# Chunk 0's decays loaded by themselves, an explicit early order, and 96-column last chunks in a chunked scan with two feed-forward layers

## The chip, the cores and the metric

The kernel runs on one core of one Trainium2 chip. The metric is device time of one execution in microseconds (us). The kernel before takes 632.46 us, the median of 3 runs (632.3 to 632.98).

## The reference, cut to what matters

Three layers follow each other; each reads the whole output of the one before.

```python
# 1. scan: 4 batches, 8 heads, 768 steps, head size 32, state size 16
la  = log(clip(a, 1e-6, 1)) ; cum = cumsum(la)           # within a chunk
M   = (C @ B.T) * exp(cum_i - cum_j) * causal
y   = M @ x + (C @ state) * exp(cum)
state = exp(sum(la)) * state + sum_j B_j x_j exp(cum_last - cum_j)
# 2. 3072 tokens of 256:  g = x @ w_gate ; v = x @ w_val ; y = (silu(g) * v) @ w_out      (1536 wide)
# 3. h = x @ w_in ; y = relu(h)**2 @ w_out                                               (2048 wide)
```

## The kernel before, in words

The 768 steps of a batch are cut into 7 chunks: six of 112 steps and a last one of 96 (Q = 112; 28 chunks in all). For each chunk the kernel makes a matrix of decay products, L (a scan on VectorE over decays that TensorE has spread over the partitions, `spread` and `scan`), the scores (`scores`, tile cb), their product mt (`times`), and the chunk's output and new state in one group of 8 matmuls (`outputs`, tile ys). Ahead of the scores the inputs B and C (tile eb) are loaded, transposed by TensorE (`transpose`, tile trb) and copied out of PSUM by ScalarE in five pieces (`copy_b`, `copy_c`, tile bct). The state goes to the next chunk by a copy, a transpose (tile turn) and another copy. The chunks of one batch hang on each other by that state.

The decays `a` lie in one tile, dv: heads on partitions, chunks and steps along the row, with a zero ahead of each chunk. Two copies of it are loaded, one at partition 0 by SyncE (SP) and one at partition 64 by ScalarE's queue (`load_a`, L254 and L258), zeroed around the edges by VectorE (`zeros`, L245 to L248) and clamped in two instructions (`clip`, L264). All chunks' decays go by one load and one clamp, and the first `spread` (tile ab, L593) waits for it.

The second layer's weights are split into a high and a low part by ScalarE, VectorE and GpSimd (tile raw to v, hi, lo); its matmuls (tiles g, v, acc) run with three products each, from L764 and L878. The third layer's are h and acc (L764, L950 and L959).

The order of all work is made on the host before the program is built. The kernel adds operations with costs, dependences and priorities to a `Graph`; `order()` plays them through an event queue, at each free engine starting the available operation of the lowest priority number, and the program is issued in that order. `PLAN["turns"]` overwrites the priorities of about 510 early operations by a table of numbers. Each engine then takes its instructions strictly in this order and waits on semaphores.

Where TensorE's next operation starts more than 150 ns after the last one in that plan, the kernel puts matmuls on a tile of zeros ahead of it (tile idle, written into the next operation's own PSUM buffer, L233: "fills"). Their number is the planned gap over 105 ns, plus 2; for the first gap of the program it is another formula with the constant COLD.

Of the kernel before, what the change touches and what calls it, by code (L numbers as in the profile page):

```python
# [16 lines left out]
ALU = mybir.AluOpType  # L17
# [10 lines left out]
class Op:  # L28
    def __init__(self, eng, cost, fn, deps, prio, bufs, lat):
        self.port, self.pieces = False, 0  # L30
        self.eng, self.cost, self.fn, self.prio, self.bufs, self.lat = eng, cost, fn, prio, bufs, lat
        self.deps = [d for d in deps if d is not None]
        self.next, self.wait, self.keep = [], 0, None


class Graph:
# [14 lines left out]
    def order(self):  # L51
# [5 lines left out]
        avail, out, events, now = {}, [], [], 850.0  # L57
        busy = {}
        for op in self.ops:
            if not op.wait:  # L60
                avail.setdefault(op.eng, []).append(op)
        left = len(self.ops)
        seq = queued = 0
        while left:
            started = True
            while started:
                started = False
                for eng, ops in avail.items():
# [4 lines left out]
                    for op in ops:  # L73
                        if best is not None and (eng == "DMA" or op.prio > best.prio):
                            continue
# [6 lines left out]
                        if op.keep and "ps" in need:  # L82
                            more, own, accs = op.keep
                            need["ps"] += more + sum(len(accs[u]) for u in own if not accs[u][0].taken)
# [4 lines left out]
                    ops.remove(best)  # L89
# [20 lines left out]
            while events and events[0][0] <= now:  # L110
# [13 lines left out]
                for o in op.next:  # L124
                    if (o.eng == op.eng) == near:
                        o.wait -= 1
                        if not o.wait:
                            avail.setdefault(o.eng, []).append(o)
# [5 lines left out]
def kernel(  # L134
# [13 lines left out]
    nc = tc.nc  # L148
# [93 lines left out]
    def zeros():  # L242
        for u in range(HG):
            w = dv_all[64 * u : 64 * u + R]
            nc.vector.memset(w[:, :, 0:1], 0.0)  # L245
            if full < NCB:
                nc.vector.memset(w[:, full, 1 + S - full * Q :], 0.0)
        nc.vector.memset(dv_all[R:64], 0.0)  # L248

    def load_a(u):  # L250
# [4 lines left out]
            out=w[:, :full, 1:], in_=v[:, : full * Q].rearrange("p (c q) -> p c q", c=full)  # L255
# [3 lines left out]

    def clip():  # L260

        w = dv_all[0 : 64 + R]
        for v in (w[:, :full, 1:], w[:, full:, 1 : 1 + S - full * Q]):
            nc.vector.tensor_scalar(v, v, 1e-6, 1.0, op0=ALU.max, op1=ALU.min)  # L264
# [67 lines left out]
    op_tab = g.add("ACT", 600, act_table, prio=-940)  # L332
# [9 lines left out]
    op_zero = g.add("DVE", 1000, zeros, prio=-960)  # L342
    ld_a = [dma(q, 2, 450, 350, lambda u=u: load_a(u), [], -950) for u, q in enumerate(["SP", "ACT"])]
    op_clip = g.add("DVE", 900, clip, [*ld_a, op_zero], -950)

    def keep_decays(b):
# [5 lines left out]
        b: dma("SP", 1, 450, 200, lambda b=b: keep_decays(b), [op_clip], 300 + b if b else 100 * PLAN["kept_at"], pieces=56)  # L352
# [109 lines left out]
    def chunk_ops(k, prio, after=(), load_after=()):  # L462
# [120 lines left out]
        if early and k < C0:  # L583
# [23 lines left out]
            o = g.add("PE", 1080, spread, [op_clip, op_pick, before.scans[-1] if before else None], prio, [*pab, c.L], lat=250)  # L607
# [87 lines left out]
        def outputs():  # L695
            ps = new(psy, [P, 512], F32, "ys")
            y = ps[:, 0:256].rearrange("p (g q) -> p g q", g=HG)
            for h in range(H):
                i, j = divmod(h, G)
                nc.tensor.matmul(  # L700
                    y[j * D : (j + 1) * D, i, :], xa[k % NX][0:K, h, :], mt[0:K, h, :],
# [393 lines left out]
    for i, at in PLAN["turns"].items():  # L1095
        g.ops[i].prio = (at, i)
# [3 lines left out]
    with tc.manual_schedule():  # L1100
        for op in order:
            fills.clear()
            if op.eng == "PE":
                if op.start < PLAN["warm"]:
# [3 lines left out]
                    if gap > 150:  # L1108
                        fills.append(int(n) + PLAN["more"])
# [40 lines left out]
    turns={  # L1150
# [97 lines left out]
```

## Time and profile before

| what | value |
|---|---|
| median of 3 runs | 632.46 us |
| the profiled execution, its own time | 635.0 us |
| its span | 633.3 us |
| TensorE (PE) busy | 628.8 us, 99% |
| VectorE (DVE) busy | 430.0 us, 68% |
| ScalarE (ACT) busy | 337.6 us, 53% |
| GpSimd (POOL) busy | 103.6 us, 16% |

The profiled execution took 1.7 us more than its span, and 2.54 us more than the median of the runs. Busy time is the share in which an engine has an instruction; a fill counts as busy TensorE like any other matmul, so 99% does not mean 99% of useful work. PEld is TensorE's weight load, which runs beside its matmuls. One matmul in full 32-bit floats stands as two matmuls in the rows (8 of them are x16). Times in the rows are counted from the start of the span.

### The profile page before, as it was taken

Reading aid. Unit: us, or ns where it says so; the run is one execution under the profiler, and the core shown is the slowest. Engines: PE = TensorE matmul, PEld = TensorE weight load, DVE = VectorE, ACT = ScalarE, POOL = GpSimd, SP = SyncE. Lnnn points to the kernel's source line nnn. Section 1 sums busy time; section 2 is a strip of 40 time slices with the busy share of each in tenths; the row PEclk is TensorE's granted clock in tenths of the full one; section 3 lists DMA queues with packets and bytes.
Section 4 is the critical chain, followed back from the end, with each engine's and each line's share of the span. In section 5 each row is a group of like instructions: output and inputs, shape, how many; then the busy total and the mean of one; then the engine's idle time right before and its main releaser. Section 6 shows DMA issues by size and latency. Waiting matters only on the chain.

```text
span 633.3 us, 9819 instructions
## 1 busy us (share of the span) xinstructions
PE 628.8 (99%) x3755; PEld 532.3 (84%) x3755; DVE 430.0 (68%) x666; ACT 337.6 (53%) x615; POOL 103.6 (16%) x130
## 2 busy tenths in 40 slices
PE   9999999999999999999999999999999999999997
PEld 7889999999787878787888888888888888888897
DVE  5888889887877768794588985455555554554543
ACT  4888896454534444553467564444444444444443
POOL 4046523231312122211033310000000000000000
PEclk9999999999999999999999999999999999999999
DMA  8879764776565646533043100020010100100201
GB/s 188 204 167 221 196 158 67 137 122 140 94 138 92 133 84 113 148 77 124 1 132 134 67 1 1 0 35 0 1 33 1 26 10 1 33 1 0 35 1 34
DMA packets 153823, 49.85 MB, mean 79 GB/s; under 512 B 141616, under 2 KB 142128, under 8 KB 153776
## 3 DMA queue, kind: packets, MB, share of 16 engines
q1 hardware_dynamic: 153232, 48.87, 35.3%
q8 instruction: 29, 0.48, 0.3%
q10 hardware_dynamic: 544, 0.36, 0.2%
q14 instruction: 18, 0.15, 0.1%
HBM read 34.96 MB, written 3.25 MB: 60 GB/s over the span
## 4 chain that ended last, share of the span: by engine, by line
PE 99%; DVE 0%; issue 0%
PE h L764 21%; PE g L764 18%; PE acc L950 17%; PE acc L878 16%; PE v L764 14%; PE acc L959 4%; PE ys L700 3%; PE cb L662 2%; PE trb L233 1%; PE cb L653 1%; PE ab L593 1%; PE ab L233 1%; PE cb L233 0%; PE g L233 0%; PE trb L506 0%; PE turn L739 0%
## 5 line engine op out<-in xcount | busy, mean ns | idle before, releaser
L940 DVE TENSOR_TENSOR p<-t,p 128x512 fp32r<-128x512 f32 x96 | 67.9, 707 | 65.7 <-ACT p L936 65.7
L933 DVE TENSOR_TENSOR t<-t 128x512 f32<-128x512 f32 x96 | 66.4, 692 | 52.1 <-ACT t L930 52.0
L936 ACT ACTIVATE p<-t 128x512 fp32r<-128x512 f32 x96 | 60.7, 632 | 75.1 <-PE acc L950 53.2
L950 PE MATMUL acc<-p,hi 128*128 128x512 f32 x320 | 98.6, 389 | 0.0
L930 ACT ACTIVATE t<-h 128x512 f32<-128x512 f32 x96 | 57.4, 598 | 67.5 <-PE h L764 64.6
L878 PE MATMUL acc<-p,hi 128*128 128x512 f32 (+3 forms) x320 | 89.9, 365 | 0.0
L828 ACT ACTIVATE t<-g 128x512 f32<-128x512 f32 (+5 forms) x88 | 45.2, 519 | 73.9 <-PE g L764 66.3
L764 PE MATMUL h<-xh_all,hi 128*128 128x512 f32 x192 | 74.8, 390 | 0.0
L764 PE MATMUL h<-xl_all,hi 128*128 128x512 f32 x192 | 74.8, 390 | 0.0
L764 PE MATMUL h<-xh_all,lo 128*128 128x512 f32 x192 | 74.7, 389 | 0.0
L851 DVE TENSOR_TENSOR p<-t,p 128x512 fp32r<-128x512 f32 (+3 forms) x80 | 57.6, 731 | 21.9 <-ACT p L846 21.3
L950 PEld LDWEIGHTS acc<-p,hi 128*128 128x128 f32 x320 | 60.1, 188 | 12.5
L846 ACT ACTIVATE p<-t 128x512 fp32r<-128x512 f32 (+3 forms) x80 | 45.5, 573 | 46.9 <-DVE t L831 37.8
L764 PE MATMUL g<-xh_all,hi 128*128 128x512 f32 (+3 forms) x184 | 65.6, 356 | 0.0
L831 DVE TENSOR_TENSOR t<-t,v 128x512 f32<-128x512 f32 (+2 forms) x68 | 43.7, 646 | 31.1 <-PE v L764 23.6
L764 PE MATMUL g<-xl_all,hi 128*128 128x512 f32 (+3 forms) x184 | 64.6, 351 | 0.0
L764 PE MATMUL g<-xh_all,lo 128*128 128x512 f32 (+3 forms) x184 | 64.6, 351 | 0.0
L878 PEld LDWEIGHTS acc<-p,hi 128*128 128x128 f32 x320 | 57.2, 189 | 7.3
L950 PE MATMUL acc<-p,lo 128*128 128x512 f32 x160 | 62.2, 389 | 0.0
L878 PE MATMUL acc<-p,lo 128*128 128x512 f32 (+3 forms) x160 | 57.9, 362 | 0.0
L764 PE MATMUL v<-xh_all,hi 128*128 128x512 f32 (+2 forms) x136 | 51.1, 376 | 0.0
L764 PE MATMUL v<-xl_all,hi 128*128 128x512 f32 (+2 forms) x136 | 51.0, 375 | 0.0
(103 smaller groups left out, 1097.3 us busy)
## 6 DMA issues: line engine op xcount, KB each, us to landing
ab<-decay SPq DMA_DIRECT2D x23, 452.0 KB, 4.2
raw<-in_moe_w_out_dram SPq DMA_DIRECT2D x14, 512.0 KB, 4.6
raw<-in_moe_w_in_dram SPq DMA_DIRECT2D x8, 512.0 KB, 4.2
raw<-in_moe_w_val_dram SPq DMA_DIRECT2D x6, 512.0 KB, 5.9
raw<-in_moe_w_gate_dram SPq DMA_DIRECT2D x6, 512.0 KB, 5.4
xa<-in_x_dram SPq DMA_DIRECT2D x24, 112.0 KB, 3.0
out_dram<-o SPq DMA_DIRECT2D x40, 64.0 KB, 1.9
bc<-in_B_dram SPq DMA_DIRECT2D x18, 56.0 KB, 2.2
```

Source lines behind the costliest of these rows:

```text
L764: nc.tensor.matmul(ps, l, r, start=(i == 0), stop=(i == len(terms) - 1))
L828: nc.scalar.activation(t[:, :n], gg(), AF.Silu)
L831: nc.vector.tensor_tensor(tb.t[:, :n], tb.t[:, :n], vv(), op=ALU.mult)
L846: nc.scalar.activation(p[:, 0, :n], tb.t[:, :n], AF.Copy)
L851: e.tensor_tensor(p[:, 1, :n], tb.t[:, :n], p[:, 0, :n].bitcast(F32), op=ALU.subtract)
L878: nc.tensor.matmul(ps, l, r, start=bank not in done_f, stop=f == NF - 1, skip_group_check=True,)
L930: nc.scalar.activation(new(tb, [P, TN], F32, "t"), ph.t, AF.Relu)
L933: nc.vector.tensor_tensor(tb.t, tb.t, tb.t, op=ALU.mult)
L936: nc.scalar.activation(new(pb, [P, 2, TN], F32R, "p")[:, 0, :], tb.t, AF.Copy)
L940: e.tensor_tensor(pb.t[:, 1, :], tb.t, pb.t[:, 0, :].bitcast(F32), op=ALU.subtract)
L950: nc.tensor.matmul(acc[-1 - i][m], l.t[:, w], pb.t[:, r, :], start=(f == 0 and s == 0), stop=(f == NF2 - 1 and s == 2),)
L959: nc.tensor.matmul(acc[-1 - i][q][:, :256], pb.t[:, l, tk], r, start=(f == 0 and s == 0), stop=(f == NF2 - 1 and s == 2),)
```

## The change: what it does

Four edits.

1. Chunk 0's decays are loaded and clamped by themselves (`load_first`, `clip_first`), zeroed by a short `zeros`; the other chunks' (`load_a`, `clip`, `zeros_rest`) follow as operations of their own. Chunk 0's `spread` waits for the first alone, all other ones for the second.
2. The table of priorities goes. In its place `PLAN["seq"]` lists the early operations of each engine in order (some 400 for VectorE, 90 for GpSimd, 320 for TensorE, 360 for ScalarE, 150 for SyncE); `order()` gives an engine the next one of its list as soon as that one can run, and the rest by priority as before. The lists also rearrange the work.
3. Where a planned gap of TensorE ends at or before 12 us of the plan, the fills are now the gap over 216 ns, plus 1. Elsewhere the formulas stay. In the built program there are 64 fills where there were 137.
4. The last chunk of each batch multiplies 96 columns in `outputs` in place of 128.

```diff
-        for u in range(HG):
-            w = dv_all[64 * u : 64 * u + R]
-            nc.vector.memset(w[:, :, 0:1], 0.0)
-            if full < NCB:
-                nc.vector.memset(w[:, full, 1 + S - full * Q :], 0.0)
-        nc.vector.memset(dv_all[R:64], 0.0)
+        nc.vector.memset(dv_all[0 : 64 + R, 0, 0:1], 0.0)
+        nc.vector.memset(dv_all[R:64, 0, 1:], 0.0)
+
+    def zeros_rest():
+        w = dv_all[0 : 64 + R]
+        nc.vector.memset(w[:, 1:, 0:1], 0.0)
...
+    def load_first(u):
+        q = nc.scalar if u else nc.sync
+        q.dma_start(out=dv_all[64 * u : 64 * u + R, 0, 1:], in_=a.rearrange("b h s -> (b h) s")[:, :Q])
...
+    def clip_first():
+        v = dv_all[0 : 64 + R, 0, 1:]
+        nc.vector.tensor_scalar(v, v, 1e-6, 1.0, op0=ALU.max, op1=ALU.min)
...
-            o = g.add("PE", 1080, spread, [op_clip, op_pick, before.scans[-1] if before else None], prio, [*pab, c.L], lat=250)
+            o = g.add(
+                "PE", 1080 if k else 2000, spread, [op_clip if k else op_clip0, op_pick, before.scans[-1] if before else None],
+                prio, [*pab, c.L], lat=250,
+            )
...
+            m = n if last else P
...
-                    y[j * D : (j + 1) * D, i, :], xa[k % NX][0:K, h, :], mt[0:K, h, :],
+                    y[j * D : (j + 1) * D, i, :m], xa[k % NX][0:K, h, :], mt[0:K, h, :m],
...
-    for i, at in PLAN["turns"].items():
-        g.ops[i].prio = (at, i)
...
-                        fills.append(int(n) + PLAN["more"])
+                        fills.append(int(n) + PLAN["more"] if free < 1200 or op.start > 12000 else int(gap / 216) + 1)
...
-    turns={
-        0: 7236.6543, 1: -999.5758, 2: -999.5961, 3: -999.6149, 4: -999.5938, 5: -999.6135, 6: -999.4071, 7: -999.5258,
...
+    seq=dict(
+        DVE=[
+            10, 0, 9, 15, 40, 41, 36, 151, 35, 37, 152, 20, 155, 156, 101, 42, 174, 175, 102, 178,
...
```

SyncE's queue at the start of the program, before (dv are the decays, xa the x of a chunk, raw a pair of weight blocks of 512 KB, eb the B and C of a chunk):

```order
L254 DMA dv<-in_a_dram 32x6x112
L258 DMA dv<-in_a_dram 32x96
L484 DMA xa_92<-in_x_dram 112x8x32
L405 DMA raw<-in_moe_w_val_dram 128x2x512
L405 DMA raw<-in_moe_w_gate_dram 128x2x512
L495 DMA eb_101<-in_C_dram 112x8x16
L495 DMA eb_101<-in_B_dram 112x8x16
L405 DMA raw<-in_moe_w_val_dram 128x2x512
```

The same queue with the change, from its first load to the first chunk's x:

```order
L428 DMA raw<-in_moe_w_val_dram 128x2x512
L265 DMA dv<-in_a_dram 32x112
L428 DMA raw<-in_moe_w_gate_dram 128x2x512
L518 DMA eb_101<-in_C_dram 112x8x16
L518 DMA eb_101<-in_B_dram 112x8x16
L428 DMA raw<-in_moe_w_gate_dram 128x2x512
L271 DMA dv<-in_a_dram 32x5x112
L275 DMA dv<-in_a_dram 32x96
L518 DMA eb_102<-in_B_dram 112x8x16
L518 DMA eb_102<-in_C_dram 112x8x16
L428 DMA raw<-in_moe_w_val_dram 128x2x512
L507 DMA xa_92<-in_x_dram 112x8x32
```

One weight block moved ahead of the decays, of which only chunk 0's stand there; B and C of chunk 0 stand at places 4 and 5 in place of 6 and 7, and the x of chunk 0 went from place 3 to place 12.

VectorE around its first scan, before (the scan, of chunk 0, writes L and is named SCALAR_TENSOR_TENSOR here; v and raw are a weight block):

```order
L245 MEMSET dv 32x7
L247 MEMSET dv 32x16
L248 MEMSET dv 32x791
L264 TENSOR_SCALAR dv<-dv 96x6x112
L264 TENSOR_SCALAR dv<-dv 96x96
L602 SCALAR_TENSOR_TENSOR L<-ab,delta 128x452
L439 TENSOR_SCALAR v<-v 128x512
L433 SCALAR_TENSOR_TENSOR raw<-raw 128x512
```

And with the change:

```order
L251 MEMSET dv 96x1
L252 MEMSET dv 32x112
L279 TENSOR_SCALAR dv<-dv 96x112
L456 SCALAR_TENSOR_TENSOR raw<-raw 128x512
L462 TENSOR_SCALAR v<-v 128x512 x2
L625 SCALAR_TENSOR_TENSOR L<-ab,delta 128x452
L456 SCALAR_TENSOR_TENSOR raw<-raw 128x512
L466 SCALAR_TENSOR_TENSOR v<-v,raw 128x512
L625 SCALAR_TENSOR_TENSOR L<-ab,delta 128x452
L284 TENSOR_SCALAR dv<-dv 96x5x112
```

The clamp of chunk 0 is one instruction of 112 columns; that of the other chunks moved behind both scans of chunk 0.

## Rows read from the trace of the kernel before

**Rows 1.** The page: busy time by engine, and the chain's shares.

```profile
PE 628.8 (99%) x3755; PEld 532.3 (84%) x3755; DVE 430.0 (68%) x666; ACT 337.6 (53%) x615; POOL 103.6 (16%) x130
...
PE 99%; DVE 0%; issue 0%
```

**Rows 2.** Waits of PE from 0 to 50 us: total, times, longest (us).

```profile
PE ab L233 <- DVE idle L215: 1.1, 1, 1.1
```

**Rows 3.** Chain that ended last, 0 to 60 us: start, duration (us), engine, tile, line.

```profile
1.14 4.02 PE ab L233 x18
5.16 1.98 PE ab L593 x16
7.14 5.09 PE trb L233 x31
12.23 0.22 PE trb L506 x2
12.44 0.33 PE ab L233 x3
12.77 1.08 PE ab L593 x16
13.85 0.76 PE cb L233 x6
14.61 1.08 PE cb L653 x16
15.69 1.96 PE trb L233 x17
...
18.95 0.57 PE ys L700 x16
...
20.61 1.42 PE trb L233 x13
...
42.89 0.54 PE cb L233 x4
```

**Rows 4.** The same chain's shares of its 60 us by line.

```profile
by line: PE g L764 20.9%; PE trb L233 14.1%; PE cb L653 12.6%; PE ab L593 10.5%; PE ab L233 7.2%; PE acc L878 6.8%; PE ys L700 6.7%; PE cb L233 4.9%; PE g L233 4.7%; PE trb L506 3.3%; PE turn L739 2.3%; PE v L764 2.0%; PE turn L233 1.5%; PE
```

**Rows 5.** Issues of 3.2 to 4.6 us: KB each, us to landing.

```profile
eb<-in_C_dram SPq DMA_DIRECT2D x1, 56.0 KB, 5.5
```

**Rows 6.** The same of 0 to 1.5 us.

```profile
dv<-in_a_dram SPq DMA_DIRECT2D x1, 84.0 KB, 2.4
```

**Rows 7.** Timeline of SP: start, duration (us), queue, line.

```profile
0.82 0.40 SPq L254 DMA_DIRECT2D dv<-in_a_dram  x1
...
3.32 0.47 SPq L495 DMA_DIRECT2D eb<-in_C_dram  x1
```

**Rows 8.** Timeline of DVE, the clamp of the decays.

```profile
3.55 0.79 DVE L264 TENSOR_SCALAR dv<-dv 96x672 f32<-96x672 f32 x2
```

**Rows 9.** Timeline of ACT, chunk 0's copies out of PSUM.

```profile
12.48 0.28 ACT L510 ACTIVATE bct<-trb 128x128 f32<-128x128 f32 x1 [2.55 <-PE trb L506]
12.65 1.08 ACT L515 ACTIVATE bct<-trb,mask 128x112 f32<-128x112 f32 x4
```

**Rows 10.** Windows: PE, PEld, DVE, ACT, POOL busy, PEclk, DMA share, GB/s.

```profile
20.00:30.00 10.00, 10.00 (x120) 8.32 (x119) 8.87 (x15) 8.98 (x26) 0.83 (x2) 1.00 0.99 272
...
0.00:50.00 50.00, 48.87 (x525) 39.40 (x526) 38.70 (x65) 35.88 (x91) 17.40 (x39) 1.00 0.81 188
```

**Rows 11.** DMA of 0 to 14 us.

```profile
DMA packets 6665, 2.76 MB, mean 197 GB/s; under 512 B 5641, under 2 KB 5641, under 8 KB 6665
```

More of the change, by code (lines that the diff above doesn't have):

```diff
@@ L29, in __init__ @@
     def __init__(self, eng, cost, fn, deps, prio, bufs, lat):
-        self.port, self.pieces = False, 0
+        self.port, self.pieces, self.listed = False, 0, False
         self.eng, self.cost, self.fn, self.prio, self.bufs, self.lat = eng, cost, fn, prio, bufs, lat
@@ L56, in order @@
         free = {p: [None] * n for p, n in self.pools.items()}
-        avail, out, events, now = {}, [], [], 850.0
+        out, events, now = [], [], 850.0
         busy = {}
+        avail = {eng: [] for eng in ("DVE", "POOL", "PE", "ACT", "SP", "DMA")}
+        lists = {eng: [self.ops[i] for i in reversed(PLAN["seq"].get(eng, []))] for eng in avail}
+        for ops in lists.values():
+            for op in ops:
+                op.listed = True
         for op in self.ops:
-            if not op.wait:
-                avail.setdefault(op.eng, []).append(op)
+            if not op.wait and not op.listed:
+                avail[op.eng].append(op)
         left = len(self.ops)
@@ L72, in order @@
                     need = {}
-                    for op in ops:
-                        if best is not None and (eng == "DMA" or op.prio > best.prio):
+                    first = lists[eng][-1:]
+                    for op in first + ops:
+                        if op.listed and op.wait:
+                            continue
+                        if best is not None and (best.listed or eng == "DMA" or op.prio > best.prio):
                             continue
@@ L81, in order @@
                                 need[b.pool] = need.get(b.pool, 0) + 1
-                        if op.keep and "ps" in need:
+                        if op.keep and "ps" in need and not op.listed:
                             more, own, accs = op.keep
@@ L88, in order @@
                         continue
-                    ops.remove(best)
+                    (lists[eng] if best.listed else ops).remove(best)
                     best.after = []
@@ L126, in order @@
                         o.wait -= 1
-                        if not o.wait:
-                            avail.setdefault(o.eng, []).append(o)
+                        if not o.wait and not o.listed:
+                            avail[o.eng].append(o)
         self.span = now
@@ L242, in zeros @@
     def zeros():
-        for u in range(HG):
-            w = dv_all[64 * u : 64 * u + R]
-            nc.vector.memset(w[:, :, 0:1], 0.0)
-            if full < NCB:
-                nc.vector.memset(w[:, full, 1 + S - full * Q :], 0.0)
-        nc.vector.memset(dv_all[R:64], 0.0)
+        nc.vector.memset(dv_all[0 : 64 + R, 0, 0:1], 0.0)
[3 more added lines that the diff above has]
+        nc.vector.memset(w[:, 1:, 0:1], 0.0)
+        if full < NCB:
+            nc.vector.memset(w[:, full, 1 + S - full * Q :], 0.0)
+        nc.vector.memset(dv_all[R:64, 1:full, 1:], 0.0)
+        if full < NCB:
+            nc.vector.memset(dv_all[R:64, full, 1 : 1 + S - full * Q], 0.0)
+    def load_first(u):
+        q = nc.scalar if u else nc.sync
+        q.dma_start(out=dv_all[64 * u : 64 * u + R, 0, 1:], in_=a.rearrange("b h s -> (b h) s")[:, :Q])
     def load_a(u):
@@ L254, in load_a @@
         q.dma_start(
-            out=w[:, :full, 1:], in_=v[:, : full * Q].rearrange("p (c q) -> p c q", c=full)
+            out=w[:, 1:full, 1:], in_=v[:, Q : full * Q].rearrange("p (c q) -> p c q", c=full - 1)
         )
@@ L258, in load_a @@
             q.dma_start(out=w[:, full, 1 : 1 + S - full * Q], in_=v[:, full * Q :])
+    def clip_first():
+        v = dv_all[0 : 64 + R, 0, 1:]
+        nc.vector.tensor_scalar(v, v, 1e-6, 1.0, op0=ALU.max, op1=ALU.min)
     def clip():
         w = dv_all[0 : 64 + R]
-        for v in (w[:, :full, 1:], w[:, full:, 1 : 1 + S - full * Q]):
+        for v in (w[:, 1:full, 1:], w[:, full:, 1 : 1 + S - full * Q]):
             nc.vector.tensor_scalar(v, v, 1e-6, 1.0, op0=ALU.max, op1=ALU.min)
@@ L331 @@
     op_bc = g.add("POOL", 2200, setup_bc, prio=-900)
-    op_tab = g.add("ACT", 600, act_table, prio=-940)
+    op_tab = g.add("ACT", 1500, act_table, prio=-940)
     def dma(eng, n, cost, move, fn, deps=(), prio=0.0, bufs=(), pieces=256):
@@ L340, in dma @@
         return o
-    op_zero = g.add("DVE", 1000, zeros, prio=-960)
-    ld_a = [dma(q, 2, 450, 350, lambda u=u: load_a(u), [], -950) for u, q in enumerate(["SP", "ACT"])]
-    op_clip = g.add("DVE", 900, clip, [*ld_a, op_zero], -950)
+    op_zero = g.add("DVE", 230, zeros, prio=-999)
+    op_zrest = g.add("DVE", 980, zeros_rest, prio=-960)
+    ld_0 = [dma(q, 1, 450, 100, lambda u=u: load_first(u), [], -955, pieces=32) for u, q in enumerate(["SP", "ACT"])]
+    op_clip0 = g.add("DVE", 190, clip_first, [*ld_0, op_zero], -955)
+    ld_a = [dma(q, 2, 450, 350, lambda u=u: load_a(u), [], -950, pieces=200) for u, q in enumerate(["SP", "ACT"])]
+    op_clip = g.add("DVE", 800, clip, [*ld_a, op_zrest], -950, port=True)
     def keep_decays(b):
@@ L351 @@
     kept = {
-        b: dma("SP", 1, 450, 200, lambda b=b: keep_decays(b), [op_clip], 300 + b if b else 100 * PLAN["kept_at"], pieces=56)
+        b: dma("SP", 1, 450, 200, lambda b=b: keep_decays(b), [op_clip, op_clip0], 300 + b if b else 100 * PLAN["kept_at"], pieces=56)
         for b in range(NB)
@@ L1149 @@
     warm=70000,
-    turns={
[65 rows of a table removed]
-    },
+    seq=dict(
+        DVE=[
[21 rows of a table added]
+        ],
+        POOL=[
[5 rows of a table added]
+        ],
+        PE=[
[16 rows of a table added]
+        ],
+        ACT=[
[18 rows of a table added]
+        ],
+        SP=[
[8 rows of a table added]
+        ],
+    ),
 )
```

131 rows, old and new, of tables (ACT, DVE, PE, POOL) are left out of this document.

## The prediction, made before the changed kernel ran

> **What bounds the kernel now.** I read the page's busy times and its chain first: TensorE is busy 99% of the span and holds 99% of the chain [rows 1]. That share includes the fills, so next come TensorE's waits in the first 50 us, where all fills stand. There is one, of 1.1 us, for the tile of zeros itself [rows 2]: whatever TensorE needs has arrived before its fills are through. The others wait for it: ScalarE stood 2.55 us for chunk 0's transposes [rows 9]. So in the early stage the fills themselves set the pace. How much time they hold is read from the chain of the first 60 us: the L233 shares are 14.1 + 7.2 + 4.9 + 4.7 + 1.5 = 32.4%, or 19.4 us [rows 4]. The largest lump is 31 fills in 5.09 us ahead of chunk 0's transposes [rows 3]; the last load these wait for was issued right behind one that went out at 3.32 us and landed 5.5 us later, at 8.8 us [rows 5, 7], while the transposes began at 12.23 us. From 43.43 us on there are no fills, and the rest is matmul behind matmul; what the early stage gives up, the end gets whole.
>
> **The clock.** A fill takes 4.02 / 18 = 223 ns at the start and 1.42 / 13 = 109 ns later [rows 3]: its 256 columns at TensorE's lower level (1.2 GHz) and at the upper one (2.4 GHz). The window rows print the granted clock as 1.00 for both [rows 10], so the fills are the better witness. With 223 and 109 ns, 31 fills in 5.09 us are about 15 of the slow and 16 of the fast kind: the rise came near 10.5 us, after TensorE had run nothing but fills since 7.14 us.
>
> **The change part by part**, against the profiled execution (635.0 us, 2.54 us over the median of the runs).
>
> *To the first outputs (ys, 18.95 us).* Step by step, with the durations of before:
> - 15 fills in place of 18: 1.14 + 15 x 0.223 = 4.5 us.
> - Chunk 0's decays. Before, the SP copy went out at 0.82 us and landed 2.4 us later, at 3.2 us [rows 6, 7]. Now a 512 KB weight block stands ahead of it: at 272 GB/s with the DMA engines 99% busy [rows 10] that is 1.9 us, so 4.3 us at the least (were the block quicker) and 5.1 us at the most; I take 4.6. Clamping took 0.79 us for two instructions of 672 and 96 columns [rows 8]; one of 112 is put at 0.3 us (0.1 to 0.5). `spread` starts at 4.9 us against 5.16: 0.3 us won, or nothing. In the page DMA: Bandwidth & Descriptors, section Queues, rings and completion order, the Trainium skill says that each DMA engine consumes a queue's descriptors in ring order; by that rule the small copy can't pass the block. The sum has it so.
> - `spread` 1.98 us at the lower clock, then 3 fills of 0.22: 7.5 us, where 31 fills took the time to 12.23.
> - B and C of chunk 0: in SP's list they stand two places earlier, without the 96 KB of all decays and the 112 KB of x ahead of them. Two issues of 0.47 us are 0.9 us, and 112 KB more at 272 GB/s 0.4 us: 8.8 - 1.3 = 7.5 us (8.8 if nothing comes of it). The transposes start at 7.5 us: 4.7 us earlier, 3.4 at the least.
> - ScalarE's copies end 1.50 us after the transposes begin (12.23 to 13.73) [rows 9]; 8 fills of 0.22 us end at 9.8. Scores at 9.9 us against 14.61 [rows 3].
> - Scores 1.08 us, then 2 fills where 17 took 1.96 us, chunk 1's transposes, 3 fills, one `spread`, 7 fills: with 1.2 us for a load that is not early enough, 9.9 + 1.1 + 1.2 + 0.2 + 0.3 + 1.1 + 0.8 = 14.6 to 14.8 us against 18.95. That is **-4.2 us** (-3.0 to -5.0).
>
> *Behind the first outputs.* Of the 19.4 us, 4.02 + 5.09 + 0.33 + 0.76 + 1.96 = 12.2 us stand ahead of ys [rows 3], so 7.3 us behind it, in 62 fills. The built program has 26 there: 2.8 us at 109 ns, 3.0 with their entries. 4.3 us of fills go. What takes their place is not shown, since TensorE never waited here; the bounds are nothing (all 4.3 won) and all of it in waits (0). The cover is thin: in 20 to 30 us VectorE is busy 8.87 and ScalarE 8.98 of 10 us, and the DMA share is 0.99 [rows 10], so other engines are near their own pace as soon as TensorE stops holding them. I take half: **-2.1 us**.
>
> *96 columns.* One `outputs` is 0.57 us [rows 3]; a quarter less over four of them is at most 0.57 us, nothing at the least; the part that streams is about three quarters: **-0.4 us**.
>
> *The clock.* Fills go from the stretch in which it rose. If it rises where the second `spread` begins instead of near 10.5 us, one group of scores (1.08 us) and some transposes and fills take twice as long. I take **+1.0 us** (0 to 3.4, the latter if it stays low to about 17 us).
>
> *Rearranging behind 50 us* is taken at nothing: TensorE has its input there before it asks, and VectorE is busy 68% of the span [rows 1]. The second clamp now stands behind both scans of chunk 0 and before the scores' products, 0.8 us; chunk 1's `spread` waits for it, behind 3 fills, and that lies inside the 1.2 us above.
>
> Sum: -4.2 - 2.1 - 0.4 + 1.0 = -5.7; 635.0 - 5.7 = 629.3, less 2.54 is 626.8 us. All ends on one side give -9.9 and +0.4, or 622.6 and 632.9.
>
> **The rivals.**
> - *The loads decide* (20%). The DMA share over the first 50 us is 0.81 [rows 10]: 40 us of transfers, which can't be squeezed much. Chunk 0's x goes out behind four weight blocks and four B and C copies, about 2.5 MB; before, 2.76 MB took 14 us [rows 11]. So x lands at 13 to 14 us, hardly before ys wants it. If x comes 1 us late and all removed fills behind ys turn into waits: -3.2 - 0.4 + 1.0 = -2.6, 629.9 us. Against: nothing waits for a load before, and landings there lie 3 us ahead of use.
> - *Nothing comes back* (13%): no waits behind ys and the clock as before, -4.2 - 4.3 - 0.4 = -8.9, 623.6 us.
> - *Slower: the lower clock* (7%). TensorE stops and starts between few fills, and the rise doesn't come. From 12.23 to 43.43 us its chain holds 31.2 us, of which 19.4 - 9.1 = 10.3 us are fills; the other 20.9 us are work that takes twice as long at the lower level. Without the clock's term the sum is -6.7; the 2.1 us of waits that it holds behind ys would be filled by the longer work. So it decides from 8.8 us of such work at the lower level on. With half of the 20.9 us: 10.4 - 2.1 - 6.7 = +1.6, or 634.1 us. For it: ahead of the rise TensorE ran nothing but fills, and most of those go. Against: at the lower level the same work leaves fewer gaps between its instructions. In TensorE: Matmul & The Clock Gate, section What's actually happening, the Trainium skill says that "the default state is throttled, and activity releases the throttle". The trace agrees as far as it goes, with 223 ns a fill at first and 109 later; by that rule it speaks against the change that it takes activity away, and this rival is its price.
> - *Waits for fills, one for one* (8%): chunk 0's decays and copies come as late as before, and the time is 632 us.
>
> **How the numbers follow.** The forecast, 626.8 us with its own range of 625 to 628.5, has 52%. Faster by over 0.2% (below 631.2 us; 0.2% is about what a measurement of this kernel can tell from no change) are the forecast, the first two rivals and a little of the rest: 0.86. Within 0.2%: 0.07. Slower: 0.07. For 8 in 10 the range runs from 624.6 to 631.0.
>
> **What would show it.** L233 rows in the chain of the first 60 us at about 10 us in place of 19.4; chunk 0's transposes near 7.5 us and the first ys near 14.7; in place of the fills, waits of TensorE for ScalarE, VectorE or a DMA, about 2 us in all behind ys. Fills of over 200 ns beyond 17 us, or score groups of 2 us, would say that the clock ate the gain; a TensorE wait for xa or eb of over 1 us that the loads did. I am wrong if the transposes of chunk 0 stay later than 9 us, or if the matmuls from 50 us on start less than 3 us earlier than before.

## The result, and the profile after

The changed kernel takes 627.54 us (median of four, 627.31 to 627.66) against 632.61 us before (632.3 to 632.98): ratio 0.9913, 95% interval 0.9894 to 0.9931. Measured once more, six times against 22, it was 627.92 against 632.94, ratio 0.9916 (0.9894 to 0.9937). The prediction said 626.8 us, within 624.6 to 631.0. The time is right; several of its terms are not, and their errors nearly cancel.

The page's busy times and its chain by engine, after; they answer to [rows 1]:

```profile
PE 619.8 (99%) x3682; PEld 525.1 (84%) x3682; DVE 424.6 (68%) x668; ACT 335.2 (54%) x615; POOL 99.4 (16%) x130
PE 98%; DMA 1%; DVE 0%; SPq 0%; issue 0%; DVEq 0%
```

TensorE is still the bound; the 73 matmuls that are gone are fills (64 in place of 137). New in the chain is 1% of DMA. The chain of the first 60 us of the kernel after (start, duration, what; L241 are the fills) answers to [rows 3]:

```profile
1.32 4.41 DMA dv<-in_a_dram
...
6.19 2.05 PE ab L616 x16
8.25 0.75 PE trb L241 x3
9.00 0.43 PE trb L529 x2
9.42 1.49 PE cb L241 x8
10.91 1.08 PE cb L679 x16
...
12.86 1.08 PE ab L616 x16
13.94 0.87 PE ys L241 x7
14.81 0.57 PE ys L727 x16
...
16.46 0.76 PE turn L241 x6
...
17.66 1.08 PE ab L616 x16
18.74 1.52 PE g L241 x13
...
22.80 1.08 PE ab L616 x16
...
25.86 0.87 PE ab L241 x7
26.73 1.08 PE ab L616 x16
...
45.46 0.47 PE ys L727 x16
```

The first ys is at 14.81 us against 18.95, and the fills in the chain add up to 6.9 us (0.75 + 1.49 + 0.33 + 0.33 + 0.87 + 0.76 + 1.52 + 0.87), where there were 19.4 [rows 4]; 15 more fills lie beside the wait for chunk 0's decays. From the first ys to the end it is 625.9 - 14.81 = 611.1 us against 633.3 - 18.95 = 614.4. TensorE's waits in the first 50 us, after:

```profile
PE ab L616 <- DVE dv L279: 1.7, 1, 1.7
PE ab L241 <- DVE idle L223: 1.1, 1, 1.1
```

Against [rows 2] one wait is new, ahead of chunk 0's `spread`; behind ys there is none.

One thing can't be read from this pair alone: the two profiled executions differ by 7.4 us (635.0 and 627.6), the medians by 5.07. The first experiment shows why.

### The profile page after: what moved, and what is told of

Its sections match the earlier page's. It is cut to its first block, busy times and chain, and to the rows that moved or that the text cites. A ratio compares the mean times of both kernels' runs of the same rounds, so it can differ in the third digit from the quotient of the medians.

```text
span 625.9 us, 9674 instructions
## 1 busy us (share of the span) xinstructions
PE 619.8 (99%) x3682; PEld 525.1 (84%) x3682; DVE 424.6 (68%) x668; ACT 335.2 (54%) x615; POOL 99.4 (16%) x130
## 4 chain that ended last, share of the span: by engine, by line
PE 98%; DMA 1%; DVE 0%; SPq 0%; issue 0%; DVEq 0%
PE h L791 21%; PE g L791 18%; PE acc L977 17%; PE acc L905 16%; PE v L791 14%; PE acc L986 4%; PE ys L727 3%; PE cb L688 2%; PE cb L679 1%; PE ab L616 1%; DMA dv<-in_a_dram 1%; PE trb L529 0%; PE g L241 0%; PE cb L241 0%; PE turn L766 0%; PE ab L241 0%
```

## The experiments

Theory "fills": the inputs come early enough, and the time falls by the fills that go. Its rivals: "waits" or "loads" (what goes as fills returns as waits), "clock" (with less to do, TensorE runs longer at its lower level), "order" (it is the rearranged lists that make fills needless). Times are medians; a ratio is to the kernel before, measured beside each run. Some executions of the kernel before take 635 us (run 1): 1 of 23 beside runs 1 to 4, 3 of 11 beside runs 5 to 8 and 8 of 22 beside runs 9 to 12. They lower a ratio by up to 0.13%. Without them its medians are 632.49, 632.59 and 632.54 us, so the times of different runs can be compared directly. `FILLS` gives the number of fills ahead of a numbered instruction group; in the changed kernel it would be 150: 15, 144: 3, 154: 8, 168: 2, 173: 3, 157: 7, 162: 6, 374: 13, 241: 7.

**1. The kernel before, unchanged.**

> The kernel before, unchanged, profiled a second time. If the first profile (635.0 us) was a late rise of the clock or an otherwise uncommon execution: about 632.6 us profiled, first ys near 18 us or the stretch behind ys about 2 us shorter than 614.4 us. If the profiler itself costs 2.4 us on this kernel: again 635.0 us, with the same rows. The timed runs against itself: 0.0 us.

632.52 us against 632.49; the profiled execution took 632.23 (span 630.5). Its chain:

```profile
1.14 3.46 PE ab L233 x18
4.59 1.08 PE ab L593 x16
5.67 3.49 PE trb L233 x31
...
12.70 1.96 PE trb L233 x17
...
15.12 1.08 PE ab L593 x16
16.20 0.57 PE ys L700 x16
...
23.01 1.08 PE ab L593 x16
...
27.06 1.08 PE ab L593 x16
```

31 fills take 3.49 us here and took 5.09 in the first profile [rows 3]; `spread` takes 1.08 and took 1.98. Fill by fill, the spacing drops from 213 to 110 ns at 3.9 us in this execution, at 10.4 us in the first. So the first ys comes at 16.20 instead of 18.95 us, earlier than was expected for it; behind it the two agree (630.5 - 16.20 = 614.3). The clock's rise, 6.5 us later, costs 2.8 us. Being profiled is not the cause, since this execution was profiled too. Of 66 executions of the kernel before in all, 13 took 634.68 to 635.26 us and the others at most 633.11. By its time, the profile that the prediction was worked out from was one of the rarer kind. What decides the kind stays open.

**2. The old order with few fills.**

```
-                if op.start < PLAN["warm"]: ...      # 18, 31, 3, 6, 17, 7, 13, ... = 137 fills
+                if op.num in FILLS:                  # FILLS = {144: 18, 138: 9, 167: 1, 148: 2}
+                    fills.append(FILLS[op.num])
```

> The kernel before with its own order of all instructions, and 30 fills instead of 137 (18, then 9, 1 and 2 ahead of chunk 0's transposes, the second spread and the scores; none later). Theory 'fills' (inputs arrive before TensorE asks, the fills alone set the pace): transposes at 9.2 us in place of 12.23, first ys near 13.5 us, and up to 7 us more behind ys: 620 to 624 us, at or below the changed kernel. Theory 'order' (the rearranged lists bring the inputs earlier; with the old lists waits take the place of fills): 629 to 632.6 us, with TensorE waits of 4 to 10 us in the first 50 us. Theory 'clock': over 632.6 us, matmuls at the lower level past 17 us.

631.86 us, ratio 0.9984 (0.9971 to 0.9998): 107 fills fewer brought 0.6 us. TensorE's waits in the first 60 us, and windows of the same kernel (stretch, length, TensorE busy, granted clock, DMA share, GB/s):

```profile
PE trb L506 <- DMA eb<-in_B_dram: 3.2, 2, 1.6
PE trb L506 <- DVE L L602: 1.8, 1, 1.8
```

```profile
12.00:14.00 2.00, 0.69 (x7) 1.00 0.72 82
...
16.00:18.00 2.00, 1.96 (x14) 0.50 0.72 117
```

With the old lists waits do take the fills' place, and behind a stretch with TensorE busy for 0.69 of 2 us the granted clock falls to 0.50, the lower level. "Fills" falls as a theory of that order.

**3. The new order with the old formula for fills.**

```
-                        fills.append(int(n) + PLAN["more"] if free < 1200 or op.start > 12000 else int(gap / 216) + 1)
+                        fills.append(int(n) + PLAN["more"])
```

> The changed kernel with the old formula for the number of fills: 19 more fills, all ahead of ys (6, 18, 5, 6 in place of 3, 8, 2, 3). Theory 'fills': 3 at 213 ns and 16 at 110 to 143 ns, +2.5 us, 630.0 us, first ys at 17.3 us. Theory 'waits' (what is late is the loads, TensorE would have waited for x or the products anyway, or regains it behind ys): +1 us or less. Theory 'clock' (more fills bring the rise earlier): +2 us or less, rise before 10 us.

629.84 us, ratio 0.996 (0.9944 to 0.9975): 19 fills cost 2.3 us by the median, as "fills" had it. Yet the six executions lie between 627.79 and 631.43, and the profiled one, the fastest, has its first ys at 14.95 us, 0.1 us later than run 9, with fills of 110 ns from 7.2 us on. This doesn't mean that the fills were free. At 109 ns the 19 are 2.1 us; what sets them off is run 9's wait for B and C (0.58 us), which they cover, and run 9's 8 fills, transposes and scores, which took 1.91, 0.66 and 1.51 us at the lower level and 1.04, 0.41 and 1.15 at the upper one (run 5; together 1.5 us). Of the longer executions there is no trace; a later rise of the clock, as in run 1, would fit them, but is not shown.

**4. The new order without the 33 late fills.**

```
+FILLS = {150: 15, 144: 3, 154: 8, 168: 2, 173: 3}
```

> The changed kernel without the 33 fills from the first ys on (7 ahead of ys, 6, 13 and 7 behind; they hold 4.0 us of TensorE's chain). Theory 'fills': TensorE's input has arrived 0.4 us or more before it asks, so nearly all of it is won: -3 to -4 us, 623.5 to 624.5 us. Theory 'waits': half of it or more returns as waits for ScalarE and VectorE: -2 to 0 us. Theory 'clock': slower than the changed kernel, matmuls at the lower level in 12 to 30 us.

626.59 us, ratio 0.9906 (0.9893 to 0.9918). The profiled execution, 625.63 us, has the last ys of the first 60 us 2.0 us earlier than the 45.46 us of after, for 4.0 us of fills:

```profile
43.47 0.47 PE ys L727 x16
```

"Waits" is nearer than "fills". The largest wait behind ys is 0.3 us, for ScalarE; the rest is in gaps too small for a row. The intervals of this ratio and of 0.9913 overlap, so a gain over the changed kernel is likely but not shown: its four executions (625.63 to 627.02) lie below all ten of the changed kernel (627.31 to 628.56), but those were not measured beside it.

**5. 24 fills ahead of chunk 0's `spread` in place of 15.**

```
-FILLS = {150: 15, 144: 3, 154: 8, ...
+FILLS = {150: 24, 144: 3, 154: 8, ...
```

> The changed kernel with 24 fills in place of 15 ahead of chunk 0's spread, so that TensorE hardly stops from 1.14 to 6.2 us (it stood still from 4.3 to 6.19). Theory 'clock' (that stop is what keeps the fills and chunk 0's spread at the lower level until about 10 us; without it the rise comes near 4 us, as in the second profile of before): spread in 1.08 us in place of 2.05, first ys at 13.5 to 14.2 us in place of 14.81, 626.0 to 627.0 us. Theory 'chance' (when the clock rises has nothing to do with the stop): the same as the changed kernel within 0.3 us, 627.5 us. Rival 'loads': the rise comes early, but TensorE then waits for B and C of chunk 0 (landed at 8.2 us) and gains nothing: 627.5 us with a wait of 0.5 us or more for eb.

627.3 us, ratio 0.9906 (0.9888 to 0.9924). TensorE's own rows (start, duration, line, tile, shape, count, idle before):

```profile
1.13 4.19 PE L241 MATMUL ab<-idle 128*128 128x256 bf16 x24 [1.13 <-DVE idle L223]
6.20 1.15 PE L616 MATMUL ab<-dv,pick 32*128 32x113 f32 x16 [0.88 <-DVE dv L279]
8.25 0.41 PE L529 MATMUL trb<-eye,eb 128*128 128x128 f32 x2 [0.47 <-DMA eb<-in_B_dram]
8.50 1.04 PE L241 MATMUL cb<-idle 128*128 128x256 bf16 x8
14.26 0.64 PE L727 MATMUL ys<-mt,xa 128*32 128x128 f32 x16
```

The rise comes at 4.1 us and holds: 8 fills at 8.5 us take 1.04 us, where run 9's take 1.91. The first ys is 0.5 us earlier than in run 9, but the profiled execution is no faster (628.19 us, the longest of its six). The lead is lost when its chain runs into a load of decays that lands at 36.8 us; the last ys of the first 60 us is at 45.88 against 45.46 us after:

```profile
31.21 5.60 DMA ab<-decay
```

"Clock" is right about the clock. About the time "loads" is nearer, though the load that takes the lead back in this profile is not the B and C that it named (their wait was 0.47 us).

**6. Chunk 0's decays first on SP.**

```
-            31, 11, 29, 142, 140, 94, 16, ...
+            11, 31, 29, 142, 140, 94, 16, ...
```

> The changed kernel with chunk 0's decays issued on SP ahead of the first weight block instead of behind it; same fills. Theory 'queue order' (the copy landed 4.4 us after its issue because of the 512 KB block ahead of it): landed at 3.2 to 3.6 us in place of 5.73, chunk 0's spread at 4.5 us in place of 6.19; transposes then bound by B and C of chunk 0 at 8.2 to 8.4 us in place of 9.0: first ys 0.5 to 1.0 us earlier, 626.5 to 627.0 us. Rival: landed as late as now, no difference, 627.5 us.

627.9 us, ratio 0.9916 (0.9899 to 0.9933): nothing. TensorE's rows:

```profile
4.45 1.20 PE L616 MATMUL ab<-dv,pick 32*128 32x113 f32 x16
...
8.02 0.66 PE L529 MATMUL trb<-eye,eb 128*128 128x128 f32 x2 [1.94 <-DMA eb<-in_B_dram]
8.47 1.91 PE L241 MATMUL cb<-idle 128*128 128x256 bf16 x8
```

`spread` starts at 4.45 us, straight behind its fills, against 6.19, so the late landing came of the block ahead of the small copy in SP's queue. The first profile after says the same: the other copy of chunk 0's decays, 14 KB too, on ScalarE's queue with no block ahead of it, landed at 3.23 us, SP's at 5.73. The wait moves to B and C of chunk 0: 1.94 us, and behind it the fills are back at 213 ns.

**7. All decays together at the front, in the new order.**

```
+    op_clip0.deps += ld_a
-            31, 11, 29, 142, 140, 94, 16, 164, ...
+            11, 16, 31, 29, 142, 140, 94, 164, ...
```

> The changed kernel, but all decays issued at the front of SP's and ScalarE's queues and chunk 0's clamp waiting for all of them: the separate load of chunk 0's decays gives nothing, the rearranged order is kept; same fills. Theory 'order' (the separate load is worth nothing by itself): dv at 3.5 to 4.2 us, B and C of chunk 0 0.5 to 0.9 us later than now, transposes near 9.0 us: 626.8 to 627.8 us, the same as the changed kernel. Theory 'split' (the separate load is what lets B, C and the weight blocks start earlier): transposes at 9.5 us or later, 628.5 to 630 us.

629.16 us, ratio 0.9935 (0.9917 to 0.9953). Its chain (line numbers one higher):

```profile
3.70 4.99 DMA eb<-in_B_dram
8.82 0.66 PE trb L530 x2
...
11.19 1.91 PE cb L680 x16
...
15.91 0.57 PE ys L728 x16
```

B of chunk 0 goes out 0.9 us later (3.70 against 2.82), the transposes start 0.6 us later than in run 9, and ys 1.1 us. The other 0.5 us is the scores at the lower level, 1.91 us against 1.44 in run 9: here fills and scores show that level up to 13 us, and whether the edit brought that about is not shown. "Split" is nearer by the time: 1.2 us over run 9 (the intervals overlap). What the separate load is shown to do is worth 0.6 us, and not by bringing the decays, whose `spread` starts later than before, but by clearing SP's queue ahead of B and C.

**8. 128 columns.**

```
-            m = n if last else P
+            m = P
```

> The changed kernel with 128 columns in the last chunks' outputs, as before. From the profile after, 0.47 us against 0.57 us for one group, four of them: +0.4 us, 627.9 us. Rival: hidden or within the noise, 627.5 us.

629.04 us, ratio 0.993 (0.9912 to 0.9948). In its profile ys starts at 16.19 us, 1.4 us later than after, where the edit doesn't reach (the granted clock is 0.50 from 8 to 14 us); from ys to the end it is 627.6 - 16.19 = 611.4 us against 611.1. So by this profile the columns are worth 0.3 us, and the rest of the 1.1 us over run 9 is put down to the clock.

**9. The changed kernel, unchanged.**

> The changed kernel, unchanged, a second time. Theory 'clock falls at the stop' (TensorE stands still from 4.3 to 6.1 us; its fills then show the lower level at 8.5 us or still do, as in four of the five profiles with that stop or a longer one behind it): executions between 627.3 and 629.4 us as in the 128-column kernel, depending on when it rises again. Theory 'fixed': 627.3 to 627.7 us as in its first four runs.

627.92 us (627.44 to 628.56): "the clock falls at the stop" had this spread. TensorE's rows of its profile (span 625.9 us), and windows around the fall:

```profile
1.13 3.38 PE L241 MATMUL ab<-idle 128*128 128x256 bf16 x15 [1.13 <-DVE idle L223]
6.04 1.15 PE L616 MATMUL ab<-dv,pick 32*128 32x113 f32 x16 [1.53 <-DVE dv L279]
8.21 0.66 PE L529 MATMUL trb<-eye,eb 128*128 128x128 f32 x2 [0.58 <-DMA eb<-in_B_dram]
8.66 1.91 PE L241 MATMUL cb<-idle 128*128 128x256 bf16 x8
14.76 0.64 PE L727 MATMUL ys<-mt,xa 128*32 128x128 f32 x16
```

```profile
7.00:8.00 1.00, 0.62 (x7) 0.94 0.83 234
8.00:9.00 1.00, 0.80 (x4) 0.50 0.96 329
...
11.00:12.00 1.00, 1.00 (x17) 0.85 0.86 270
```

TensorE stands 1.53 us for the decays, runs 1.6 us at the upper level, stands 0.58 us for B, and the granted clock falls at 8 us and is back near 11.3. In the first profile after, it had not risen before 10.5 us; the first ys is the same. Run 3, with the second stop filled, and run 5, with the first cut to 0.88 us, have no fall; runs 4 and 8, with both stops, and run 6, with a single one of 1.94 us, have it. That is one profile each, so the stops go with the fall, and why it comes is not shown. How long it lasts differs too: with the same two stops the clock was back near 11.3 us here and near 14.4 in run 8.

**10 and 11. Fills at the early stops, none from ys on.** Run 10 joins 4 and 5; run 11 has chunk 0's decays first and

```
+FILLS = {150: 15, 144: 18, 154: 11, 168: 2, 173: 3}
```

> The changed kernel with 24 fills ahead of chunk 0's spread and none from the first ys on (both edits of earlier runs together). If they add up: -1.0 us for the removed late fills on top of 627.3 us, 626.0 us or, with the 2.0 us that the profile of that edit showed, 625.3 us. Rival 'loads': behind ys the decays of a chunk (landed 36.8 us in the profile with 24 fills) already end the wait, so that removing fills there gives nothing: 627 us.

> The changed kernel with chunk 0's decays issued first, 18 fills between its spread and its transposes (3 before, and then a wait of 1.9 us) and 11 ahead of the scores, none from the first ys on. Theory 'clock': TensorE runs through from 1.14 us, the rise at about 4 us holds (fills of 109 ns at 8 to 10 us in place of 213), transposes at 8.1 us, scores at 9.9, first ys at 13.3 to 14.0 us: 625 to 626 us. Theory 'chance': fills of 213 ns return at 8 us all the same, 627 us.

626.43 and 626.44 us, but with four executions of the 18 between 633.59 and 634.88 (ratios 0.9923, 0.9889 to 0.9956, and 0.9909, 0.9872 to 0.9945). The mean granted clock of those four is 0.980 to 0.984, of the others 0.992 to 1.000. Run 11, TensorE and windows:

```profile
8.44 1.36 PE L241 MATMUL cb<-idle 128*128 128x256 bf16 x11
14.83 1.08 PE L727 MATMUL ys<-mt,xa 128*32 128x128 f32 x16 [1.44 <-DMA xa<-in_x_dram]
```

```profile
14.00:16.00 2.00, 1.17 (x18) 0.67 0.88 75
16.00:18.00 2.00, 2.00 (x17) 0.50 0.89 315
```

The clock holds through 8 us as "clock" had it, but ys waits 1.44 us for x, starts no earlier than after (14.83 us; 13.3 to 14.0 was expected), and behind that wait the clock falls. Run 10's profile (628.32 us) is alike: ys waits 0.57 us for x, and the granted clock is 0.50 from 16 to 20 us. Its median lies between "add up" (626.0) and "loads" (627). No version here is shown to beat the changed kernel.

**12. The rearranged order alone**: runs 7 and 8's edits together, with run 3's numbers of fills.

> The changed kernel's rearranged order alone: all decays loaded together at the front and clamped ahead of chunk 0's spread, fills by the old formula (83), 128 columns. If the parts add up, undoing them costs 1.6 + 2.3 + 0.4 us: 631.8 us, so that the order alone is worth 0.7 us. Theory 'order carries it' (the others are small beside it): 629.0 to 630.5 us.

631.0 us, ratio 0.9962 (0.9949 to 0.9975): 1.9 us of the 5.0 come from the order alone (1.5 of 4.6 against the commoner executions of before), between the two theories. TensorE's rows:

```profile
8.61 0.66 PE L530 MATMUL trb<-eye,eb 128*128 128x128 f32 x2 [2.34 <-DMA eb<-in_B_dram]
9.06 4.05 PE L241 MATMUL cb<-idle 128*128 128x256 bf16 x18
```

Here the parts meet: in the wait for B the granted clock goes down (0.68 from 7 to 8 us, 0.50 from 8 to 14), and the 18 fills behind it take 4.05 us. Undone one at a time, the other parts are 2.3 us (fills), 1.2 (separate load) and 0.3 (columns); with the order that is 5.3 to 5.7 us against 4.6 to 5.1 measured, a difference within the noise.

## Why the prediction came out right, and where it was wrong

**The ladder to ys** was -4.2 us; it is 18.95 - 14.81 = -4.14 between the two first profiles. Its steps were less exact: the decays landed at 5.73 us, not 4.6 (bounds 4.3 to 5.1), and the transposes began at 9.00 us in place of 7.5, since TensorE stood for decays and ran at the lower level; 9 us was the prediction's own line for being wrong. The 1.2 us allowed behind the scores for a late load was not called on, and made up for it. That the ladder ends where it was put is in part luck. In DMA: Bandwidth & Descriptors, section Queues, rings and completion order, the Trainium skill has the ring order that the prediction leaned on; run 6 agrees, with `spread` 1.7 us earlier once the copy stands first.

**The offset of 2.54 us is the first step that failed.** The prediction took the profiled execution's excess over the median as lying outside the sum. It lay inside: it is the clock's late rise (10.4 us instead of 3.9), in the very stretch that the ladder prices. Against the commoner execution (run 1) the ladder is worth 16.20 - 14.81 = 1.4 us. Up to ys, run 9 against run 1: fills 7.0 us against 10.0 (3.46 + 3.49 + 0.33 + 0.76 + 1.96), so -3.0 (3.4 + 0.4 + 1.7 + 0.3 + 0.3 + 0.9 in run 9); one `spread` fewer, -1.1; two waits, +1.53 + 0.58; scores and transposes at the lower clock, +0.5. That is -1.5, and 1.4 was measured.

**The clock**, +1.0 us (0 to 3.4), was the right term in the wrong place. Against the first profile it is nothing. Against run 1, whose fills and `spread` are at the upper level from 3.9 us, the new kernel is at the lower one up to 10.5 us or again from 8 to 11.3. That eats what the ladder had promised beyond 1.4 us. The rival of a lower clock, 634.1 us, didn't come in the changed kernel. Four executions of runs 10 and 11, 633.6 to 634.9 us, look like it by their mean clock, but there is no trace of them. In TensorE: Matmul & The Clock Gate, section What's actually happening, the Trainium skill calls the length of the slow start "run-variable"; the 3.9 and 10.4 us of one kernel bear that out. The same section of the Trainium skill has the transition point vary by 500 ns either way; the 6.5 us measured here are far more, and the measurement decides.

**Behind ys**, half of the 4.3 us of fills was to return as waits, and with the columns -2.5 us was forecast. It was 611.1 - 614.4 = -3.3 us. The term of waits, 2.1 us, measured nothing: no wait of TensorE came behind ys. Of the fills 7.3 - 3.15 = 4.15 us went, the columns gave 0.4 (0.47 against 0.57 us, four times), and 1.08 us came back as chunk 2's `spread`. In run 1 three `spread`s stand ahead of the first ys (the third at 15.12 us) and two behind; after, two ahead and three behind (17.66, 22.80, 26.73 us). The ladder had counted it as gone; nowhere was it paid for. Waits that did not come and a `spread` that was not counted are the second step that failed. -4.15 - 0.4 + 1.08 = -3.5; the other 0.2 us lies in no row. Of the last 33 fills about half does come back when they go (run 4).

**The sum**: against the first profile -4.14 - 3.3 = -7.4 us instead of -5.7, and no offset of 2.54 instead of one. Errors of 1.7 and 2.5 us of opposite sign leave 0.8 us by the profiles, 0.7 by the medians. That the forecast came so near is luck; the way of the change and its rough size were reasoned.

**"Loads decide"** was put at 20% and shows as the next bound: x landed at 13.9 us in the first profile after, within the 13 to 14 us of that rival, and at 14.7 in run 11, and B and C of chunk 0 hold the transposes at 8.0 to 8.8 us in every profile of runs 4 to 12.

**What the prediction gave to the fills alone belongs to fills and order together**: fewer fills in the old order bring 0.6 us (run 2), the order with more fills 1.5 to 1.9 (run 12), the whole change 4.6 to 5.1.

## What to carry to other kernels

Take a second profile before working out a change to a start-up stretch: if the profiled execution stands off the median, the difference may lie in the terms that the sum prices. An instruction that is moved behind a milestone is no gain until it is paid for on the other side. Filler work is worth cutting down to what covers the waits that remain, once the order brings the inputs early. Below that, the granted clock fell behind the waits (runs 2, 10 and 11), and a median that was 1.5 us better came with 4 executions of 18 that took 7 to 8.5 us more.

## What was not expected of the hardware

The moment of the clock's rise differs by 6.5 us (3.9 and 10.4 us) between executions of one unchanged kernel whose TensorE runs through from 1.14 us. The windows print a granted clock of 1.00 for stretches whose fills take 213 ns (0 to 4 us in every profile here); there the spacing of equal matmuls is the witness. In run 9 the clock fell behind two stops of 1.53 and 0.58 us, with 1.6 us of work at the upper level between them.
